# A pause in the routing of overflow and skip lists, and an earlier start of the row scales

## The chip, the core and the metric

The kernel runs on one core of a Trainium2 chip. Its engines work side by side, each through its own list of instructions in the order written: TensorE (PE, with its weight loads PEld), VectorE (DVE), ScalarE (ACT), GpSimd (POOL), and SyncE (SP), which issues most transfers. The metric is the device time of one execution in microseconds; lower is better.

## The reference

A causal filter of seven taps over `x` (4 sequences of 3584 tokens, 192 channels, one softmaxed filter per group of 24 channels) is followed by two mixtures of eight experts, each choosing one expert per token:

```python
x = attn_out.reshape(B * S, D)                 # 14336 rows of 192
do_compute = x @ w_skip > 0                    # layer 1 handles about half of the rows
xc = x[do_compute]
e_idx = np.argmax(xc @ w_gate, axis=1)
h = np.maximum(xc[mask] @ w1[e], 0.0)          # 192 -> 1024, per expert e
y[mask] = gate_w[mask, None] * (h @ w2[e])     # 1024 -> 192
out[do_compute] = xc + y                       # the other rows skip layer 1
logits = x @ w_gate + modality_bias[modality_id]
out[mask] = gate_w[mask, None] * (np.maximum(x[mask] @ w1[e], 0.0) @ w2[e])   # layer 2, all rows
```

## The kernel before

First a phase filters the tokens and computes the gates. Rows are then handled in **blocks** of 128 rows that share an expert: a block gathers its rows from DRAM by a list of indices, transposes them, and multiplies them with the expert's two weight matrices. Blocks 0 to 55 serve layer 1 from lists that are ready early; blocks 56 to 61 serve layer 1's overflow (rows of experts with more than 896 rows); then come blocks of layer 2, first those of the rows that skipped layer 1, then the rest.

`Ffn.run` writes the blocks one after another. In iteration i PE gets the two halves of the first product of block i (`mm1`, parts p0 and p1, 20 matmuls each into one bank) and then the second product of block i-1 (`mm2`, 24 matmuls). After each `mm1` part ACT writes `hh` (the relu, in 16 bits) and DVE writes `hlo` (what the 16 bits lost). After `mm2` DVE writes the row's result into `x2a` (blocks 0 to 15) or `x2s` (later ones). Once `late_pools` has run, some blocks earlier, three banks take turns for `mm1` (`m.ph`), two for `mm2`. So p1 of block b can only start when the `hlo` of p0 of block b-1 has been read out of the same bank, and `mm2` of block b-1, in iteration b, needs that block's second `hlo`.

Between these parts `bg(i, pt)` runs at four points of an iteration (pt 0, 2, 3, 4). It sets `step[0] = i` and calls `tick()` on three lists of background tasks. A task is a generator: `yield n` lets n ticks pass before its next piece is written into the engines' lists. The order on PE, DVE, ACT and POOL is the order of writing (`InOrder`); on SP a scheduler places the transfers. Background tasks in the blocks at issue:

- `route2` (list `tk`), on DVE but for a few matmuls. `ranks` counts skip rows by expert, `choose` ranks layer 2's experts (tile `sel`, on which the second conversion lane below waits). Then come the position arithmetic: `slots`, `left`, `place` (tiles `ns`, `sz`, `st`, `rC`, `pos`), `table` (`esl`, `tab`), the overflow positions (`codeA` with `rB`), `qsl` (`pi` to `q`), and `invert`, which turns positions into the index lists by comparisons (`oa`, `ob`) and groups of 8 matmuls. Its lists are needed from block 56 on.
- two lanes of `prep` (list `tkw`), which convert the next experts' weights to a 16-bit part and a 16-bit rest. DVE's shares are eight rows per expert: four 128x512 and four 128x384, written to `o` (layer 2) or `w1b`, `w2b` (layer 1).
- `scales` (list `tk2`): for each four blocks `scale2` has DVE find the rows' maxima (`mx` twice, `s`, `ef`), POOL scale two small tiles, and, four ticks later, ACT scale four tiles.

Of the kernel before, what the change touches and what calls it, by code (L numbers as in the profile page):

```python
# [30 lines left out]
EA = 4  # L31
SA = 3
SB = 7
NSA = E * SB
XA = 16
# [80 lines left out]
class Moe:  # L116
# [654 lines left out]
        for w in self.invert(S, q, sl, pool, ob, tag, res, lp, lag, base, val):  # L771
            yield w

    def route2(self, ra, pool, ob, l1, lb, lag):
        nc, cp = self.nc, self.cp
        code, rk = self.code[:, 0, :], ra["rk"]
        r, o, r1 = [], [], []
        for w in self.ranks(self.code[:, 1, :], pool, 1, r):
            yield w
        for w in self.choose(r[3], pool):  # L780
            yield w
        for w in self.slots(r[3], NP2B, True, pool, o):
            yield w
        self.left(r[3], NS2B, True, o, "B", pool, lb, cp)
        for w in self.place(r, NP2B, o, pool, 128.0 * NS1):
            yield w
        for w in self.table(NS2B, NP2B, o, "B", pool, ob, lb, cp, NSEL - 1):
            yield w
        lim = float(SB * 128)
        ov = pool.tile([128, 8], F32, name="th")  # L790
        nc.vector.tensor_scalar(ov, ra["base"], -lim, 0.0, ALU.add, ALU.max)
        for w in self.slots(ov, 0, False, pool, r1):
            yield w
        self.left(ov, NS1, False, r1, "1", pool, l1, cp)
        for w in self.table(NS1, 0, r1, "1", pool, ob, l1, cp):
            yield w
        of = pool.tile([128, 8], F32, name="dl")
        nc.vector.tensor_scalar(of, r1[1][:, 0], 128.0, 1.0 - lim, ALU.mult, ALU.add)
        df = pool.tile([128, 8], F32, name="sb")
        nc.vector.tensor_copy(df[:, 7:8], of[:, 7:8])  # L800
        nc.vector.tensor_tensor(df[:, 0:7], of[:, 0:7], of[:, 1:8], ALU.subtract)
        yield 1
        t = pool.tile([128, 2, NT], F32, name="rB")
        p1 = rk
        for e in range(8):
            nc.vector.scalar_tensor_tensor(t[:, e % 2], code, 8.0 - e, df[:, e:e + 1].to_broadcast([128, NT]), ALU.is_ge, ALU.mult)
            nc.vector.tensor_tensor(p1, p1, t[:, e % 2], ALU.add)
            if e % 2:
                yield 1
        nc.vector.scalar_tensor_tensor(p1, code, 0.0, p1, ALU.is_gt, ALU.mult)  # L810
        nc.vector.scalar_tensor_tensor(code, p1, 128.0 * NS1, code, ALU.is_gt, ALU.mult)
        nc.vector.scalar_tensor_tensor(p1, p1, 128.0 * NS1, p1, ALU.is_le, ALU.mult)
        nc.vector.tensor_tensor(p1, p1, o[4], ALU.add)
        yield 1
        q, sl = self.qsl(p1, pool)
        nc.gpsimd.memset(self.codeA[:, 0:NT], 0.0)
        yield 1
        res = {}
        for w in self.invert(NS1 + NS2B, q, sl, pool, ob, "m", res, cp, lag):
            yield w  # L820
        for l, a, b in ((l1, 0, NS1), (lb, NS1, NS1 + NS2B)):
            l.update(idx=res["idx"][:, a:b], va=res["va"][:, a:b])
# [477 lines left out]
def build(tc, x, cw, m1w1, m1w2, mod, bias2, m2w1, m2w2, wgs, out):  # L1300
    with ExitStack() as ctx:
        m = Moe(tc, ctx)
# [7 lines left out]
        rt = ctx.enter_context(tc.tile_pool(name="rt", bufs=1))  # L1310
        ob = m.oa = ctx.enter_context(tc.tile_pool(name="ob", bufs=4))
        pw = ctx.enter_context(tc.tile_pool(name="pw", bufs=2))
        pq = ctx.enter_context(tc.tile_pool(name="pq", bufs=4))
        la, ls, l1, lb, l2, lr = {}, {}, {}, {}, {}, {}
        ra = dict(a=la, s=ls)
# [12 lines left out]
        step, scaled = [-1], [0]  # L1328
# [25 lines left out]
        def routes():  # L1354
            while "idx" not in ls:
                yield 1
            va = m.cp.tile([128, NSA], F32, name="va")
            ra["va"] = va
            k = 0
            while k < NSA:  # L1360
                c = order[k][0] * SB + order[k][1]
                n = 1
                while k + n < NSA and order[k + n][0] * SB + order[k + n][1] == c + n:
                    n += 1
                nc.gpsimd.tensor_copy(va[:, k:k + n], ls["va"][:, c:c + n])
                k += n
                yield 1
            for i in m.route2(ra, rt, ob, l1, lb, 3):
                yield i

        tk, tk2, tkw = Tasks(), Tasks(), Tasks()
# [3 lines left out]
        def phase1():  # L1375
            v = next(gp, None)
            if v == 1:
                nc.sync.dma_start(rows[0:128, :], m.dz.bitcast(I32))
                nc.sync.dma_start(rows2[0:128, :], m.dz.bitcast(I32))
            if v == 2:  # L1380
                tkw.add(lane(0))
            if routed[0] < p1.codes:
                tk.add(m.route_a(routed[0], m.code[:, 0, :], rt, ob, ra))
                routed[0] += 1
            return v
# [17 lines left out]
        def late_pools():  # L1403
            st.close()
            m.py.append(m.py2)
            m.ph.append(m.ph3)
            px = ctx.enter_context(tc.tile_pool(name="px", bufs=1))
            w["x"] = px.tile([128, NC - XA, D], F32, name="x2s")
            po = sp.enter_context(tc.tile_pool(name="po", bufs=1))
            pw2 = sp.enter_context(tc.tile_pool(name="pw2", bufs=2))  # L1410
            w["pw2"] = pw2
            tkw.add(lane(1))
            o = po.tile([128, 4, F], F16, name="o1"), po.tile([128, W2C + 2], F16, name="o2")
            w["o"] = o
            tk.add(routes())
# [4 lines left out]
        def scales():  # L1420
            for c in range(0, NC, NB1):
                nb = min(NB1, NC - c)
                while step[0] < c + nb + 3:
                    yield 1
                for k in ffn.scale2(x2of(c, nb), mt[:, c:c + nb, :], nb):
                    yield k
                scaled[0] = c + nb

        def posts(par):
            for c in range(par * NB1, NC, 3 * NB1):  # L1430
                nb = min(NB1, NC - c)
                va = ra["va"][:, c:c + nb] if c < NSA else l1["va"][:, c - NSA:c - NSA + nb]
                while scaled[0] < c + nb:
                    yield 1
                for k in ffn.post(x2of(c, nb), mt[:, c:c + nb, :], nb, va, rows2[128 + c // GT * 2048:2176 + c // GT * 2048, :].rearrange("(p t) c -> p t c", p=128)[:, c % GT:c % GT + nb, :], m.codeA[:, c:c + nb]):
                    yield k
# [25 lines left out]
        def bg(i, pt):  # L1462
            step[0] = i
            if "x" not in w:
                phase1()
                if p1.codes == NG:
                    while phase1() is not None:
                        pass
                    late_pools()
            if i == XA and pt == 0:  # L1470
                tk2.add(scales())
            if i == n1 - 6 and pt == 4:
                tk.drain()
                tkw.drain()
                sp.close()
                ffn.pg = ctx.enter_context(tc.tile_pool(name="pg", bufs=2))
                ffn.pw = pw
                m.ph.pop()
                ffn.late = ctx.enter_context(tc.tile_pool(name="pl", bufs=4))
            if i == n1 + 2 and pt == 0:  # L1480
                tk.add(posts(0))
            if i == n1 + 4 and pt == 2:
                tk.add(posts(1))
            if i == n1 + 6 and pt == 4:
                tk.add(posts(2))
            if n1 + 7 < i < n2 - 6 and not tk.live and "idx" not in l2:
                tk.add(m.route(m.codeA[:, 0:NC], NS2A, "2", rt, ob, l2, np=NP2A, perm=True, top=NSEL - 1))
            if i == n2 and pt == 0:
                w["any"] = m.cp.tile([128, 1], I32, name="any")
                nc.vector.tensor_tensor(w["any"], l1["nrem"], lb["nrem"], ALU.add)  # L1490
                for v in (l2["nrem"], lb["un"], l2["un"]):
                    nc.vector.tensor_tensor(w["any"], w["any"], v, ALU.add)
                nc.vector.tensor_scalar(w["any"], w["any"], 1, None, ALU.min)
            if i == n2 - 6 and pt == 0:
                tk.drain()
                if "idx" not in l2:
                    tk.add(m.route(m.codeA[:, 0:NC], NS2A, "2", rt, ob, l2, np=NP2A, perm=True, top=NSEL - 1))
                    tk.drain()
            if i < n2:
                for _ in range(2 if i < EA * SA and "idx" not in ls else 1):  # L1500
                    tk.tick()
                tkw.tick()
                tk2.tick()
# [79 lines left out]
```

## Time and profile before

| | |
|---|---|
| median of three runs | 1000.76 us (1000.63 to 1001.26) |
| profiled execution: time, span of the core | 1001.09 us, 999.3 us |
| busy: PE, DVE, POOL, ACT | 917.8, 591.2, 512.7, 475.5 us |
| mean granted clock of TensorE | 0.967 |

Busy time is the sum of an engine's instructions; PE's matmuls are pipelined, so a busy PE is one that has no gap, not one at its peak. The profiled execution stands 0.33 us above the median of the runs. On DVE an instruction's end is recorded a little after the next one has begun, so what an instruction takes from the engine is read from start to start. Times in the trace count from the start of the span.

### The profile page before, as it was taken

What the parts mean: (1) busy time and instruction counts of PE and PEld (TensorE: products, weight loads), DVE (VectorE), ACT (ScalarE), POOL (GpSimd) and SP (SyncE); (2) the same over time, 40 slices, a digit from 0 to 9 for tenths busy, and PEclk for the clock granted to TensorE, in tenths of its full rate; (3) what the DMA queues carried; (4) which work ended last, traced back from release to release, by engine and by line L of the source; (5) the groups of instructions that cost most, each with busy time, mean ns of one, the idle gap of its engine ahead of it and who ended that gap; (6) DMA issues with size and microseconds to landing.
All of it is one profiled execution on the core that took longest, in us unless ns stands there. A gap on an engine that the chain in (4) does not pass through costs nothing. (4 is left out here: it accounts for less than half of the span.)

```text
span 999.3 us, 28862 instructions
## 1 busy us (share of the span) xinstructions
PE 917.8 (92%) x11000; PEld 852.6 (85%) x11000; DVE 591.2 (59%) x1624; ACT 475.5 (48%) x895; POOL 512.7 (51%) x985
## 2 busy tenths in 40 slices
PE   6999868997999999979999999999999999999993
PEld 4666668987999999968888898898888999999993
DVE  5689977899798877534455555477432333333330
ACT  3877743545686654324555555432233333333331
POOL 4155543742646355444768777644444555555431
PEclk9999859999999999999999999999999999999997
DMA  9595576764969776589333433322493232232240
GB/s 316 193 332 191 186 205 184 196 137 129 238 183 245 216 223 197 162 236 326 73 94 107 101 90 106 115 70 61 96 314 66 73 73 70 74 73 74 74 122 15
DMA packets 106196, 150.77 MB, mean 151 GB/s; under 512 B 80591, under 2 KB 85689, under 8 KB 100800
## 3 DMA queue, kind: packets, MB, share of 16 engines
q1 hardware_dynamic: 91424, 119.34, 38.8%
q0 software_dynamic: 13920, 28.87, 12.6%
q8 instruction: 88, 1.44, 0.6%
q14 instruction: 60, 0.49, 0.2%
q10 hardware_dynamic: 704, 0.63, 0.2%
HBM read 174.22 MB, written 51.08 MB: 225 GB/s over the span
## 5 line engine op out<-in xcount | busy, mean ns | idle before, releaser
L71 PEld LDWEIGHTS <-w1b 128*128 128x128 f16 x4840 | 371.4, 99 | 41.9 <-issue 13.5
L71 DVE SCALAR_TENSOR_TENSOR ws<-bank,ws 128x512 f16<-128x512 f32 x220 | 151.4, 690 | 262.1 <-ACT ws L71 215.1
L71 PE MATMUL bank<-xp,w1b 128*128 128x256 f16 x2200 | 266.5, 275 | 4.4 <-DMA xp<-gt 2.7
L71 PE MATMUL bank<-w2b,ws 128*128 128x192 f16 x2640 | 239.6, 246 | 0.1
L71 PEld LDWEIGHTS <-ws 128*128 128x128 f16 (+2 forms) x2696 | 223.6, 98 | 2.5
L71 POOL DMA_INDIRECT out_dram<-u,si x114 | 115.5, 1014 | 174.7 <-ACT ws L71 61.8
L71 ACT ACTIVATE ws<-bank 128x512 f16<-128x512 f32 x220 | 130.7, 598 | 105.5 <-PE bank L71 83.8
L71 PE MATMUL bank<-xt,w1b 128*128 128x128 f16 x2640 | 165.7, 223 | 11.5 <-DVE hlo L71 7.3
L71 ACT ACTIVATE hh<-bank 128x512 f16<-128x512 f32 x132 | 78.4, 594 | 151.7 <-PE bank L71 145.5
L71 PE MATMUL bank<-w2b,hh 128*128 128x192 f16 x1056 | 140.4, 249 | 4.7 <-DMA w2b<-s2a 3.5
L71 PE MATMUL bank<-w2b,hlo 128*128 128x192 f16 x528 | 131.4, 249 | 0.6 <-DVE hlo L71 0.6
L71 ACT ACTIVATE u<-bank,c 128x192 f32<-128x192 f32 x114 | 48.1, 422 | 165.3 <-PE bank L71 139.8
L71 DVE SCALAR_TENSOR_TENSOR hlo<-bank,hh 128x512 f16<-128x512 f32 x132 | 89.9, 684 | 56.5 <-ACT hh L71 51.3
L71 PEld LDWEIGHTS <-hh 128*128 128x128 f16 x1056 | 95.9, 100 | 5.4 <-issue 5.1
L71 POOL DMA_INDIRECT gt<-rows,idxm x62 | 62.4, 1007 | 10.8 <-issue 6.4
L71 POOL TENSOR_TENSOR xs<-gt 128x128 f32<-128x128 f16 x124 | 53.0, 449 | 27.8 <-DVE x2a L71 13.0
L71 POOL DMA_INDIRECT gt<-rows,idx x58 | 57.4, 989 | 14.3 <-issue 8.1
L71 PE MATMUL bank<-xg,band 128*112 128x384 f32 x128 | 58.1, 542 | 1.6 <-DVE hl L71 1.6
L71 ACT COPY xtb<-bank 128x672 f16<-128x672 f16 x64 | 45.9, 719 | 18.8 <-PE bank L71 18.6
L71 POOL TENSOR_SCALAR ef<-ef 128x4 f32<-128x4 f32 (+1 forms) x16 | 4.4, 276 | 97.3 <-DVE ef L71 97.2
L71 PEld LDWEIGHTS <-hlo 128*128 128x128 f16 x528 | 52.3, 99 | 1.6 <-DVE hlo L71 0.8
L71 POOL DMA_INDIRECT gt<-rows,idxs x44 | 47.3, 1075 | 6.7 <-POOL c L71 4.1
(293 smaller groups left out, 1137.2 us busy)
## 6 DMA issues: line engine op xcount, KB each, us to landing
w1b<-s1b SPq DMA_DIRECT2D x59, 1024.0 KB
w2b<-s2b SPq DMA_DIRECT2D x59, 768.5 KB
xg<-in_x_dram SPq DMA_DIRECT2D x7, 1536.0 KB
rows<-hl SPq DMA_DIRECT2D x7, 1386.0 KB
ws<-in_moe_w_dram SPq DMA_DIRECT2D x12, 768.0 KB
s1a<-w1b SPq DMA_DIRECT2D x8, 1024.0 KB
w1b<-s1a SPq DMA_DIRECT2D x7, 1024.0 KB
s2a<-w2b SPq DMA_DIRECT2D x8, 768.5 KB
```

Source lines behind the costliest of these rows:

```text
L71: r = f(*args, **kw)
```

## The change

`route2` stops between `choose` and `slots`: it yields once per tick until block 13 is reached. `scales` is added to its list at block 12 (`EA * SA`) rather than 16 (`XA`). Nothing is added to or taken from the work.

```diff
-    def route2(self, ra, pool, ob, l1, lb, lag):
+    def route2(self, ra, pool, ob, l1, lb, lag, step):
...
         for w in self.choose(r[3], pool):
             yield w
+        while step[0] < 13:
+            yield 1
         for w in self.slots(r[3], NP2B, True, pool, o):
             yield w
...
-            for i in m.route2(ra, rt, ob, l1, lb, 3):
+            for i in m.route2(ra, rt, ob, l1, lb, 3, step):
...
-            if i == XA and pt == 0:
+            if i == EA * SA and pt == 0:
                 tk2.add(scales())
```

DVE's list before, where `choose` ends and `slots` begins (`sel` is the last row of the one, `ns` the first of the other; the `x2a` row is the result of block 8, written in iteration 9):

```order
L71 TENSOR_REDUCE key<-rB 128x8
L71 TENSOR_SCALAR sel<-key 128x8
L71 TENSOR_SCALAR ns<-off 128x8
L71 TENSOR_SCALAR ns<-ns 128x8 x2
L71 CAST sz<-ns 128x8
L71 TENSOR_TENSOR sz<-ns 128x8
L71 TENSOR_TENSOR rB<-gt_3236,sz 128x64 x2
L71 SCALAR_TENSOR_TENSOR x2a<-bank_60,c,xs 128x192
```

DVE's list now, from the result of block 10 on (the first `hlo` row here belongs to block 12, the last one to p0 of block 13):

```order
L71 SCALAR_TENSOR_TENSOR x2a<-bank_60,c,xs 128x192
L71 SCALAR_TENSOR_TENSOR hlo<-bank_58,hh 128x512
L71 TENSOR_REDUCE mx<-x2a 128x4
L71 SCALAR_TENSOR_TENSOR hlo<-bank_59,hh 128x512
L71 TENSOR_SCALAR mx<-mx 128x4
L71 TENSOR_SCALAR s<-mx 128x4
L71 TENSOR_SCALAR ef<-mx 128x4
L71 SCALAR_TENSOR_TENSOR x2a<-bank_64,c,xs 128x192
L71 SCALAR_TENSOR_TENSOR hlo<-bank_63,hh 128x512
L71 TENSOR_SCALAR ns<-off 128x8
L71 TENSOR_SCALAR ns<-ns 128x8 x2
L71 CAST sz<-ns 128x8
```

`ns` follows `sel` at once before; now it stands behind the first `hlo` of block 13, four blocks later, and a group of scale rows stands in block 12.

The other end of the position arithmetic, on DVE before (the `hlo` row is p1 of block 16; `o` is a row of weight conversion):

```order
L71 SCALAR_TENSOR_TENSOR hlo<-bank_58,hh 128x512
L71 SCALAR_TENSOR_TENSOR codeA<-code,codeA 128x128
L71 SCALAR_TENSOR_TENSOR code<-codeA,code 128x128
L71 SCALAR_TENSOR_TENSOR codeA<-codeA 128x128
L71 TENSOR_TENSOR codeA<-codeA,pos 128x128
L71 SCALAR_TENSOR_TENSOR o_2517<-ws_3331,wsc,o_2517 128x2x192
```

and now (the first `hlo` row is p0 of block 20, the second p1; the `x2s` row is the result of block 18):

```order
L71 SCALAR_TENSOR_TENSOR x2s<-bank_60,c,xs 128x192
L71 SCALAR_TENSOR_TENSOR codeA<-code,codeA 128x128
L71 SCALAR_TENSOR_TENSOR code<-codeA,code 128x128
L71 SCALAR_TENSOR_TENSOR codeA<-codeA 128x128
L71 TENSOR_TENSOR codeA<-codeA,pos 128x128
L71 SCALAR_TENSOR_TENSOR hlo<-bank_59,hh 128x512
L71 TENSOR_SCALAR pi<-codeA 128x128
L71 TENSOR_SCALAR si<-pi 128x128
L71 TENSOR_SCALAR sl<-si 128x128
L71 TENSOR_SCALAR pi<-pi 128x128
L71 CAST q<-pi 128x128
L71 SCALAR_TENSOR_TENSOR hlo<-bank_63,hh 128x512
```

Before, the arithmetic runs from iteration 9 to iteration 17 and three conversion rows lie within it. Now it runs from iteration 13 to iteration 20. From the `hlo` of p0 of block 13 to that of p0 of block 20, both included, DVE's list now holds all position arithmetic up to the last `codeA` row, 15 `hlo` rows, 7 rows of `x2a` and `x2s`, eight conversion rows of 128x512 and eight of 128x384 (two whole experts), and three groups of scale rows. The conversions stand in the same blocks as before. The first group of `invert` matmuls on PE moves from iteration 20 to 24; there are 16 groups in either kernel.

## Rows read from the trace of the kernel before

**Rows 1.** Busy time by stretch: start and end, length, busy time per engine, granted clock, DMA.

```profile
190.00:262.00 72.00, 64.08 (x916) 63.00 (x917) 67.70 (x202) 36.80 (x64) 31.78 (x74) 0.98 0.67 179
250.00:425.00 175.00, 175.00 (x2549) 175.00 (x2547) 137.29 (x298) 103.52 (x194) 94.10 (x216) 1.00 0.74 209
```

**Rows 2.** Waits from 193 to 262 us: us in total, times, longest.

```profile
POOL ef L71 <- DVE ef L71: 20.5, 3, 12.1
...
PE bank L71 <- DVE hlo L71: 7.9, 5, 3.9
```

**Rows 3.** Timeline of PE: start, length, operation, count, wait ahead of it.

```profile
193.43 2.40 PE L71 MATMUL bank<-xt,w1b 128*128 128x128 f16 x40
197.65 2.40 PE L71 MATMUL bank<-xt,w1b 128*128 128x128 f16 x40
...
210.78 1.28 PE L71 MATMUL bank<-xt,w1b 128*128 128x128 f16 x20
...
242.12 1.28 PE L71 MATMUL bank<-xt,w1b 128*128 128x128 f16 x20 [3.92 <-DVE hlo L71]
...
246.87 2.40 PE L71 MATMUL bank<-xt,w1b 128*128 128x128 f16 x40
...
256.23 1.28 PE L71 MATMUL bank<-xt,w1b 128*128 128x128 f16 x20
257.35 1.08 PE L71 MATMUL bank<-ob,oa 128*128 128x62 f16 x8
258.25 1.30 PE L71 MATMUL bank<-xt,w1b 128*128 128x128 f16 x20
```

**Rows 4.** Timeline of DVE, same columns.

```profile
195.38 0.69 DVE L71 SCALAR_TENSOR_TENSOR hlo<-bank,hh 128x512 f16<-128x512 f32 x1 [0.59 <-ACT hh L71]
...
197.96 0.16 DVE L71 TENSOR_SCALAR ns<-off 128x8 int32<-128x8 f32 x1
...
237.12 0.61 DVE L71 SCALAR_TENSOR_TENSOR o<-ws,wsc,o 128x384 f16<-128x384 f32 x1
237.65 0.16 DVE L71 TENSOR_SCALAR mx<-mx 128x4 f32<-128x4 f32 x1
...
238.00 0.22 DVE L71 TENSOR_SCALAR pi<-codeA 128x128 int32<-128x128 f32 x1
...
239.23 0.61 DVE L71 SCALAR_TENSOR_TENSOR o<-ws,wsc,o 128x384 f16<-128x384 f32 x1
...
241.39 0.68 DVE L71 SCALAR_TENSOR_TENSOR hlo<-bank,hh 128x512 f16<-128x512 f32 x1
241.99 0.80 DVE L71 SCALAR_TENSOR_TENSOR o<-ws,wsc,o 128x512 f16<-128x512 f32 x1
242.71 0.68 DVE L71 SCALAR_TENSOR_TENSOR hlo<-bank,hh 128x512 f16<-128x512 f32 x1
...
262.37 0.42 DVE L71 SCALAR_TENSOR_TENSOR x2s<-bank,c,xs 128x192 f32<-128x192 f32 x1 [0.86 <-POOL c L71]
```

**Rows 5.** DVE's groups by form, 197.96 to 237.12 us: count, busy us, mean ns, idle.

```profile
L71 DVE SCALAR_TENSOR_TENSOR hlo<-bank,hh 128x512 f16<-128x512 f32 x14 | 9.5, 680 | 0.0
L71 DVE SCALAR_TENSOR_TENSOR x2a<-bank,c,xs 128x192 f32<-128x192 f32 x7 | 2.9, 411 | 0.0
...
L71 DVE SCALAR_TENSOR_TENSOR o<-ws,wsc,o 128x512 f16<-128x512 f32 x2 | 1.5, 746 | 0.0
...
L71 DVE TENSOR_REDUCE mx<-x2a 128x4 f32<-128x768 f32 x1 | 0.9, 943 | 0.0
L71 DVE SCALAR_TENSOR_TENSOR o<-ws,wsc,o 128x384 f16<-128x384 f32 x1 | 0.6, 609 | 0.0
```

**Rows 6.** The stretch with the lowered clock, columns as in the first group.

```profile
240.00:250.00 10.00, 7.88 (x95) 7.60 (x95) 9.97 (x20) 5.12 (x9) 4.51 (x10) 0.83 0.75 247
```

**Rows 7.** PE's waits for transfers from 425 to 465 us, around blocks 57 to 61.

```profile
PE bank L71 <- DMA xt<-gt: 4.1, 2, 2.5
PE bank L71 <- DMA w2b<-s2a: 3.5, 2, 2.6
```

## The prediction

> **What bounds the kernel now.** I read the busy time by stretch first. From 250 to 425 us PE has no gap at all, 175.00 us busy in 175 [rows 1]: there the kernel costs what its matmuls cost, and whatever is late at 250 is as late at 425. From 190 to 262 us it is different. PE is busy for 64.1 of 72 us and DVE for 67.7 [rows 1]. The waits of that stretch say why: PE waited five times for DVE's `hlo`, 7.9 us together [rows 2]. The timeline of DVE then shows how full it is: after a wait of 0.59 us ahead of the `hlo` row at 195.38, the next idle time that it names comes ahead of the row at 262.37 [rows 4]. Between these, DVE is the bound, and a stretch of its list takes as long as its rows take.
>
> A block costs PE 4.22 us (193.43 to 197.65, the starts of two blocks) [rows 3]. DVE's own share of a block, two `hlo` rows of 0.60 us from start to start (241.39 to 241.99 [rows 4]) and one `x2a` row of at most 0.41 us [rows 5], is 1.6 us. So about 2.6 us per block are free on DVE for the background, and the question is what each block gets.
>
> **What the change moves.** Nothing is added or removed; two pieces of DVE work change place. The position arithmetic leaves iterations 9 to 12 and starts in iteration 13, and the scale groups start four blocks earlier. The weight conversions stay where they are, from iteration 14 on. So the pause takes work off four blocks in which DVE had little else, and lays it over blocks that already carry two experts' conversions and now three groups of scale rows. I price the new stretch as one sum, from the `hlo` of p0 of block 13 to that of p0 of block 20, because the order shows that it ends with the last `codeA` row just ahead of that `hlo`.
>
> The base is the trace's own stretch from the `ns` row at 197.96 to the `o` row at 237.12 [rows 4]: 39.16 us without idle time, in which all the position arithmetic ran, with 14 `hlo`, 7 `x2a`, three conversion rows and one `mx` row among it [rows 5]. The new stretch has the same arithmetic and the same 7 results. It differs by:
>
> - one more `hlo` (15 for 14): +0.6 us;
> - six more conversion rows of 128x512 (eight for two) at 0.72 us (241.99 to 242.71) and seven more of 128x384 (eight for one) at 0.53 us (237.12 to 237.65) [rows 4]: 4.3 + 3.7 = +8.0 us;
> - scales: three groups, each an `mx` of 0.94 us [rows 5] and three small rows of 0.35 us (237.65 to 238.00 [rows 4]), less the one `mx` in the base: 3.9 - 0.9 = +2.9 us. With rows from start to start it would be a little less, so I take 2.7.
>
> Sum: 39.2 + 0.6 + 8.0 + 2.7 = 50.5 us.
>
> **From DVE's sum to PE's time.** Up to block 13 PE had no wait for DVE: it starts block 13 at 210.78 [rows 3], and the pause changes nothing ahead of that but makes DVE lighter. With DVE no longer behind, the first `hlo` of a block starts 1.95 us after the block (195.38 against 193.43 [rows 3, 4]), so the stretch starts at 212.7 and ends at 212.7 + 50.5 = 263.2. What it holds up is p1 of block 21, which uses the same bank. Before, such a start followed its `hlo` by 0.13 us (242.12 after 241.99 [rows 3, 4]), so p1 of block 21 starts at 263.3.
>
> Before, p1 of block 21 started at 258.25. But two groups of `invert` matmuls had run by then (iterations 20 and 21 to 22) that now come later, 0.90 us each (257.35 to 258.25 [rows 3]). They must still be done, so the fair mark is 258.25 - 1.8 = 256.45, and the delay is 263.3 - 256.45 = 6.9 us. The second `hlo` of block 20 stands five `pi` to `q` rows later, 1.23 us (238.00 to 239.23 [rows 4]) plus its own 0.60; PE needs only 1.12 us (256.23 to 257.35 [rows 3]) before it wants it for `mm2`. That adds 0.7. After this DVE's list is light (the `invert` rows with a block of `hlo`, no conversion until iteration 23), so the sum ends: **+7.6 us**.
>
> Sorted by PE: before, it lost 7.9 us waiting and 1.65 us at the lowered clock (half of `mm1` and `mm2` took 4.75 us, 242.12 to 246.87, where 4.22 - 1.12 = 3.10 is normal [rows 3]). Now it loses about 17 us, all of it between block 15 or 16 and block 21, and none in blocks 12 to 14.
>
> What costs nothing: the earlier scale rows on ACT, busy for 36.8 of 72 us [rows 1]; and POOL's `ef` rows, which wait for DVE and hold up the gathers behind them. POOL once stood 12.1 us for one `ef` [rows 2], and no wait of PE for a gather shows in that stretch; if that cover were gone, a gather late by 2 us would cost 2 us once. The end of `invert` moves from iteration 44 to 47, with its lists first wanted around iteration 52: five blocks, some 21 us, of slack.
>
> Both ends of what I can't see: the rows of the sum, priced by one row of their kind each, might be off by 1 us together either way; the clock could fall again in the last of the waits, +1.65 us; and part of the loss may be absorbed by the waits for transfers after 425 us, 4.1 + 3.5 = 7.6 us [rows 7]. I take none of these, since PE's releases of weight buffers start those transfers, so they move with PE. The likeliest case reaches from +4.5 to +10.
>
> **Time.** The profiled execution took 1001.09 us, 0.33 over the median, so 1001.1 + 7.6 = 1008.7 there, and 1000.76 + 7.6 = **1008.4 us** as a median.
>
> **Rivals.**
>
> *Faster: the pause clears the waits and the stacked work finds room.* For it: the first of the five waits fall into blocks that get lighter. The decision point is the price of the stretch: at 50.5 - 7.6 = 42.9 us the kernel stays the same, below it gains, at most the 7.9 + 1.65 = 9.6 us that are lost now, which gives 991.2. Against it: the position arithmetic alone with its blocks' own rows took 39.2 us in this trace without a gap, and the eleven us added to it are rows with prices. Chance 6%.
>
> *No change: the loss is taken back.* If the transfers waited for after 425 us were on their way regardless of PE, a PE that comes 7.6 us late would find them landed, and the 7.6 us of waits [rows 7] would go: 1000.8. Against it: in the code each of these weight loads goes into a buffer that an earlier block must have left. Chance 9%.
>
> *Worse: the clock.* In the stretch from 240 to 250 us, after the longest waits, the granted clock was 0.83, a mix of the two levels of 1.2 and 2.4 GHz; between 250 and 425 us, with PE always busy, it was 1.00 [rows 1, 6]. In the new stretch PE would be at work only some 60% of the time for about 40 us. If it ran at 1.2 GHz through blocks 16 to 21, a block would take 8.44 us, more than the 7.2 us that DVE takes (50.5 over seven blocks). Six such blocks from 223.4 (210.78 + 3 x 4.22) end at 274.0, where the forecast has block 22 start at 267.2 (263.3, 1.12, 0.7 and `mm2`, 4.22 - 2 x 1.12 = 2.0): 6.8 us more, 1015.2. Against it: a PE at 1.2 GHz would be the slower engine, would have no waits and, as after 242, get its clock back. Chance 10%. The Trainium skill (TensorE: Matmul & The Clock Gate, What's actually happening) says that the throttled clock is the default and that activity releases it, which is the rule behind this rival; this trace agrees as far as it goes, with 0.83 after waits and 1.00 in unbroken work.
>
> The pause doing nothing is excluded by the order, in which `ns` stands four blocks later.
>
> **How the numbers follow.** 0.2% is 2.0 us, about what a measurement of this kernel can tell from no change. The forecast has 72%, the clock 10%, no change 9%, faster 6%, and 3% stay for a partial loss under 2 us or a partial gain. Slower by over 0.2%: 72 + 10 and a little, 84%; within 0.2%: 9%; faster: 7%. The range 1003.5 to 1012.0 holds the forecast with its bounds (1005.3 to 1010.8) and some of a partial absorption or of a clock that stays low for two or three blocks; the rest, about 2 in 10, is left out.
>
> **What the new profile would show.** PE without a wait for `hlo` from 193 to about 222 us; from there to about 266 us a row of waits for `hlo`, two per block, most of 0.5 to 3 us, about 17 us together (less where the clock falls). DVE with idle time in blocks 9 to 12 and none from 213 to about 266. Block 22 starting near 267, where 258.25 + 1.12 + 2.0 gives 261.4 before. PE full from there to about 432, and the same waits of 7 to 8 us for transfers after it, 7 to 8 us later. I would be wrong if DVE has idle time between 215 and 260, if the waits after 425 shrink by what was lost before, or if the clock is 0.5 for more than a few us there.

## The result, and the profile after

The changed kernel is slower, by more than forecast. Its six runs took 1010.96 to 1020.35 us, with a median of 1017.17 us; the kernel before took 1001.14 us beside them (median of six). The ratio, formed like all ratios here from undisturbed runs (which leaves out one run of `a_half`), is 1.0145 with a 95% interval of 1.0111 to 1.0178, which is 14.5 us; the forecast was 7.6 us, in a range that ended at 1012.0. Runs of one kernel on one chip spread by about 1% here (988.63 to 998.69 us in 23 runs of the kernel before), and chips differ by as much (medians of the kernel before from 993.26 to 1004.48 us), so a kernel is compared only with the kernel before measured beside it. The change was measured three more times: 1.0130 (1.0093 to 1.0166), 1.0135 (1.0102 to 1.0167) and 1.0107 (1.0064 to 1.0150).

The profiled execution took 1014.88 us, with a span of 1013.1 us and a mean granted clock of 0.965 (0.967 before). The busy time by stretch answers to [rows 1] and [rows 6], with the same columns:

```profile
190.00:262.00 72.00, 58.69 (x844) 57.46 (x845) 61.11 (x182) 34.95 (x64) 26.92 (x68) 0.98 0.59 157
212.00:264.00 52.00, 36.69 (x515) 35.46 (x513) 49.83 (x150) 24.80 (x45) 19.10 (x45) 0.96 0.47 122
250.00:260.00 10.00, 9.62 (x121) 9.27 (x119) 9.69 (x31) 1.79 (x3) 0.00 (x0) 0.83 0.83 229
260.00:270.00 10.00, 6.11 (x74) 5.92 (x72) 9.68 (x27) 7.46 (x15) 7.83 (x17) 0.83 0.91 294
270.00:430.00 160.00, 159.12 (x2299) 158.76 (x2297) 123.47 (x265) 90.33 (x164) 79.82 (x183) 1.00 0.66 191
```

PE is busy for 58.7 of 72 us where it was busy for 64.1. From 212 to 264 us DVE is busy for 49.8 of 52 us and PE for 36.7: DVE is the bound there; from 270 to 430 us it is PE again, busy for 159.1 of 160 us. The clock is lowered in two slices, where it was in one. The waits of PE from 193 to 300 us, and from 425 to 465 us, answer to [rows 2] and [rows 7]:

```profile
PE bank L71 <- DVE hlo L71: 15.5, 7, 3.9
PE bank L71 <- DVE wsc L71: 0.5, 1, 0.5
...
PE bank L71 <- DMA w2b<-s2a: 3.2, 2, 2.2
PE bank L71 <- DMA xt<-gt: 2.7, 2, 2.5
PE bank L71 <- DMA w1b<-s1b: 0.2, 1, 0.2
```

The waits for `hlo` have gone from 7.9 to 15.5 us. Those for transfers are 6.1 us in place of 7.6 here, but 8.1, 5.7 and 8.4 us in three further traces of the changed kernel and 7.6 us in a second one of the kernel before: they did not shrink as a rule. Where the waits stand is in PE's timeline (to [rows 3]):

```profile
226.65 1.28 PE L71 MATMUL bank<-xt,w1b 128*128 128x128 f16 x20 [1.66 <-DVE hlo L71]
...
234.53 1.28 PE L71 MATMUL bank<-xt,w1b 128*128 128x128 f16 x20 [3.51 <-DVE hlo L71]
...
249.51 1.86 PE L71 MATMUL bank<-xt,w1b 128*128 128x128 f16 x20 [2.42 <-DVE hlo L71]
254.25 2.40 PE L71 MATMUL bank<-xt,w1b 128*128 128x128 f16 x40
...
264.19 2.29 PE L71 MATMUL bank<-xt,w1b 128*128 128x128 f16 x20 [3.89 <-DVE hlo L71]
268.66 2.40 PE L71 MATMUL bank<-xt,w1b 128*128 128x128 f16 x40
```

The first wait is that of p1 of block 16, the last that of p1 of block 21, and block 22 starts at 268.66. Before, it started at 261.37:

```profile
261.37 1.84 PE L71 MATMUL bank<-xt,w1b 128*128 128x128 f16 x30
```

Behind the last wait 20 matmuls took 2.29 us where 1.28 is usual, in a slice with a granted clock of 0.83. From 249.51 to 254.25 are 4.74 us where 3.10 are usual, in the other such slice. That the clock fell because PE had stood is tested below. DVE's timeline has both ends of the stretch that the prediction summed (to [rows 4]):

```profile
212.60 0.69 DVE L71 SCALAR_TENSOR_TENSOR hlo<-bank,hh 128x512 f16<-128x512 f32 x1 [0.51 <-ACT hh L71]
...
263.46 0.68 DVE L71 SCALAR_TENSOR_TENSOR hlo<-bank,hh 128x512 f16<-128x512 f32 x1
264.06 0.21 DVE L71 TENSOR_SCALAR pi<-codeA 128x128 int32<-128x128 f32 x1
...
432.63 0.69 DVE L71 SCALAR_TENSOR_TENSOR hlo<-bank,hh 128x512 f16<-128x512 f32 x1 [0.52 <-ACT hh L71]
```

From the row at 212.60 on, the next idle time that the timeline of DVE names is 0.87 us ahead of a row at 270.82. From 212.60 to 264.06 are 51.46 us (50.5 in the sum), with the rows that the sum counted (to [rows 5]):

```profile
L71 DVE SCALAR_TENSOR_TENSOR hlo<-bank,hh 128x512 f16<-128x512 f32 x15 | 10.2, 681 | 0.5 <-ACT hh L71 0.5
...
L71 DVE SCALAR_TENSOR_TENSOR w1b<-ws,wsc,w1b 128x512 f16<-128x512 f32 x4 | 3.2, 794 | 0.0
L71 DVE SCALAR_TENSOR_TENSOR o<-ws,wsc,o 128x512 f16<-128x512 f32 x4 | 3.0, 753 | 0.0
...
L71 DVE TENSOR_REDUCE mx<-x2a 128x4 f32<-128x768 f32 x3 | 2.8, 946 | 0.0
```

The row at 432.63 is `hlo` of p0 of block 56, by which the same work is done in both kernels. **The mark of block 56** in what follows is the start of that row less the start of the `hlo` of p0 of block 8, ahead of anything that is changed. It stands at 231.12 us before and at 241.73 after: 10.61 us. The other rows of the two marks, two from before and one from after:

```profile
190.92 0.67 DVE L71 SCALAR_TENSOR_TENSOR hlo<-bank,hh 128x512 f16<-128x512 f32 x1
422.04 0.69 DVE L71 SCALAR_TENSOR_TENSOR hlo<-bank,hh 128x512 f16<-128x512 f32 x1 [0.52 <-ACT hh L71]
```

```profile
190.90 0.67 DVE L71 SCALAR_TENSOR_TENSOR hlo<-bank,hh 128x512 f16<-128x512 f32 x1
```

In three further traces of the changed kernel it is 10.68, 10.86 and 10.81 us, in a second one of the kernel before 0.03: unlike the whole time, this part repeats within 0.3 us.

### The profile page after: what moved, and what is told of

Its sections match the earlier page's. It is cut to its first block, busy times and chain, and to the rows that moved or that the text cites. A ratio compares the mean times of both kernels' runs of the same rounds, so it can differ in the third digit from the quotient of the medians.

```text
span 1013.1 us, 28858 instructions
## 1 busy us (share of the span) xinstructions
PE 921.4 (91%) x11000; PEld 855.4 (84%) x11000; DVE 593.2 (59%) x1624; ACT 475.2 (47%) x895; POOL 512.2 (51%) x985
## 5 line engine op out<-in xcount | busy, mean ns | idle before, releaser
L71 POOL DMA_INDIRECT gt<-rows,idxm x62 | 62.4, 1007 | 10.8 <-issue 6.2
```

The costliest lines, as they stand in the source:

```text
L71: r = f(*args, **kw)
```

## The experiments

All of them, with the mark of block 56 against the kernel before, the time (median, or a single run), that of the kernel before measured beside it, and the ratio:

| kernel | what it is | block 56, us | time | before | ratio (95%) |
|---|---|---|---|---|---|
| e1_pause_only | the pause alone | +9.04 | 1006.08 | 993.26 | 1.0126 (1.0089 to 1.0162) |
| e2_scales_only | the early scales alone | +3.78 | 999.04 | 993.26 | 1.0071 (1.0046 to 1.0096) |
| r_after | the changed kernel again | +10.68 | 1005.92 | 993.26 | 1.0130 (1.0093 to 1.0166) |
| p2b12 | no pause, half pace in blocks 12 to 25, scales from 24 | -6.47 | 989.21 | 993.26 | 0.9950 (0.9922 to 0.9977) |
| b_again | the kernel before again | +0.03 | 1003.66 | 1001.28 | single run |
| a_fill912 | changed, four DVE rows more in blocks 9 to 12 | +12.00 | 1016.62 | 1001.28 | single run |
| a_fill1720 | changed, four DVE rows more in blocks 17 to 20 | +12.68 | 1014.49 | 1001.28 | single run |
| a_warm | changed, matmuls in the waits | +9.75 | 1011.15 | 1001.28 | 1.0107 (1.0066 to 1.0147) |
| a_half | changed, route at half pace up to block 27 | +0.33 | 1008.07 | 1002.72 | 1.0035 (1.0006 to 1.0063) |
| v_p2b10 | no pause, half pace in blocks 10 to 25, scales from 24 | -4.61 | 999.02 | 1002.72 | 0.9971 (0.9947 to 0.9996) |
| v_p19 | the pause alone, until block 19 | +11.84 | 1020.96 | 1002.72 | single run |
| r2_after | the changed kernel again | +10.86 | 1014.51 | 1002.72 | 1.0135 (1.0102 to 1.0167) |
| b_delay22 | before, 190 matmuls more in blocks 22 to 31 | +13.24 | 1004.48 | 994.89 | 1.0098 (1.0067 to 1.0130) |
| b_delay44 | before, 190 matmuls more in blocks 44 to 53 | +10.65 | 1002.93 | 994.89 | 1.0080 (1.0045 to 1.0114) |
| r3_after | the changed kernel again | +10.81 | 1006.87 | 994.89 | 1.0107 (1.0064 to 1.0150) |
| v_p2b10m | v_p2b10, clearing of codeA later | -4.06 | 999.03 | 1004.48 | 0.9949 (0.9925 to 0.9973) |
| v_p2b10e | v_p2b10, clearing and ef rows later | -5.36 | 984.38 | 993.64 | 0.9909 (0.9877 to 0.9942) |

**Which edit.** Each half of the change alone (diffs from the changed kernel: first the pause is kept, then the scales), and the change again.

```diff
-            if i == EA * SA and pt == 0:
+            if i == XA and pt == 0:
```

> The pause until block 13 alone; the row scales begin at block 16 as before. Stacked rows (the ledger of DVE): two of the three scale groups leave the stretch from block 13 to block 20, so it is about 1.2 to 2.6 us shorter than in the changed kernel; block 22 starts near 267 us (268.66 with both edits) and the time is 1 to 3 us under that of the changed kernel of the same call, some 12 us over the kernel before. Rival, the earlier scales are the cause: the time is within 3 us of the kernel before.

```diff
-        while step[0] < 13:
-            yield 1
```

> The earlier row scales alone, no pause. Stacked rows: two scale groups of about 2 us each come into blocks 12 to 16, where DVE has the position arithmetic already and is behind; PE's waits for hlo grow by about 2 us and the time by 2 us, to 1003. Rival, the earlier scales are the cause of most of the loss: 1010 or more, with waits of ACT or POOL that the kernel before does not have.

> The changed kernel once more, for its spread. If its runs fall into two groups by themselves (1011 to 1015 and about 1020, as in the six runs so far), they do so again, with the mean granted clock lower by 0.006 to 0.01 in the upper group. Rival, the two groups were chance of one chip: one group near 1012 or near 1020.

The pause does most of it: 9.0 of 10.6 us at block 56, 1.6 us less than with both edits, as expected (1 to 3); over the whole program the two did not differ (1006.08 and 1005.92 us). The scales alone cost 3.8 us, more than the 2 us expected. In their traces PE waits for `hlo` for 14.0 and 10.2 us:

```profile
PE bank L71 <- DVE hlo L71: 14.0, 7, 3.4
```

```profile
PE bank L71 <- DVE hlo L71: 10.2, 5, 3.2
```

For the scales that is 2.3 us more than before, near the 2 us that were put for their rows, and the clock is lowered in two slices (0.83 from 230 to 240 us and from 240 to 250 us) where it was in one. PE waits for neither ACT nor POOL there. Over the whole program the scales alone cost 4.6 to 9.5 us by their interval, more than the 3.8 us at block 56; where the rest is lost was not traced. The two halves do not add up to the whole (12.8 us): both fill the same blocks. The two groups of times in the first six runs of the changed kernel (1011 to 1015 and about 1020 us) did not come again: 1003.69 to 1009.52 us without a gap.

**What a DVE row costs, by place.** Four rows more on DVE (in-place, without effect on the data):

```diff
+            if i in (17, 18, 19, 20) and pt == 0:
+                q = m.iq[:, 0:64, :].rearrange("p a b -> p (a b)")
+                nc.vector.scalar_tensor_tensor(q.rearrange("p (c t) -> p c t", c=4), m.identf.unsqueeze(1).to_broadcast([128, 4, 128]), 0.0, q.rearrange("p (c t) -> p c t", c=4), ALU.mult, ALU.add)
```

> The changed kernel with four rows of 128x512 more on DVE, one in each of the blocks 9 to 12; they leave their target as it was. Stacked rows: DVE stands idle there for about a microsecond per block, so rows of 0.7 us cost nothing: block 22 within 0.4 us of the changed kernel. Rival, DVE's total work sets the time: 2.9 us later.

> The changed kernel with the same four rows in the blocks 17 to 20. Stacked rows: DVE has no idle time there, so each row costs its price: block 22 is 2.7 to 2.9 us later than in the changed kernel, plus or minus a drop of the clock more or less (1.5 us). Rival, PE is held back by the clock or by something else than DVE: less than 1 us.

> The kernel before once more, for a trace from the chip of the other runs. All theories: waits for hlo near 8 us between 190 and 300 us, block 22 near 261 us, one drop of the clock in that stretch.

In blocks 17 to 20 the four cost 2.07 us at block 56 (12.68 - 10.61, one trace). In DVE's timeline the first of them takes 0.60 us from start to start, so their price is 2.4, not the 2.7 to 2.9 that was expected:

```profile
240.16 0.68 DVE L71 SCALAR_TENSOR_TENSOR iq<-identf,iq 128x512 f16<-128x512 f32 x1
240.76 0.21 DVE L71 TENSOR_TENSOR esl<-esl,e 128x56 f32<-128x56 f32 x1
```

In blocks 9 to 12 they cost 1.39 us, where nothing was expected. Three show no cost: PE's blocks 9 to 13 start as in the changed kernel (3.41 us later each, and so is block 8). The one in block 12 was not; it comes ahead of the `mx` row there, and DVE's first `hlo` of block 13 starts at 216.80, 0.79 us later than by that offset. So block 12, just ahead of the full stretch, had no room left. The direction is as expected, but the two placements differ by only 0.7 us, in one trace each.

**The clock in the waits.**

```diff
+                for _ in range({16: 24, 17: 48, 18: 24, 19: 24, 21: 48}.get(i, 0)):
+                    nc.tensor.matmul(self.m.spare, self.m.ident, self.m.ident, start=True, stop=True)
                 self.mm1(X[k], jb["b"], 2 * part + 1, H[k])
```

> The changed kernel with 24 or 48 matmuls of 128x128 on PE more (1.3 or 2.7 us by 0.056 us each), on a bank that nothing reads, ahead of p1 of the blocks 16 to 19 and 21, where the changed kernel waits 1.7 to 3.9 us: PE works through the waits, the waits end when they did. If the drops of the clock in that stretch (near 250 and 264 us, about 3 us together) come of PE's standing still, they go: the granted clock stays 1.00 from 220 to 280 us, block 22 starts 1.4 to 3 us earlier and the time falls by as much. Rival, the clock drops for another reason or at fixed times: the drops stay and block 22 is where it was or later.

Two slices of its trace, and from its timeline the last wait:

```profile
250.00:260.00 10.00, 8.13 (x121) 7.79 (x119) 9.65 (x33) 2.06 (x4) 0.14 (x1) 1.00 0.99 271
260.00:270.00 10.00, 8.78 (x141) 8.66 (x139) 9.76 (x25) 8.63 (x19) 8.06 (x19) 1.00 1.04 314
```

```profile
263.77 1.28 PE L71 MATMUL bank<-xt,w1b 128*128 128x128 f16 x20 [1.22 <-DVE hlo L71]
```

Where the changed kernel has 0.83 twice, the clock is 1.00: the drops came of PE's standing still. The Trainium skill (TensorE: Matmul & The Clock Gate, What's actually happening) says that the throttled clock is the default and that activity releases it; this pair of traces agrees. The gain is 0.86 us at block 56 (9.75 for 10.61), not 1.4 to 3. Inside the stretch that DVE bounds, a faster PE only reaches its next wait earlier, so what counts is the drop behind the last wait (0.65 us, see below). The second trace of the changed kernel, `r_after`, bears this out: it has a third, deeper drop, from 230 to 240 us, and its mark of block 56 is the same within 0.1 us (10.68).

```profile
230.00:240.00 10.00, 6.50 (x64) 6.15 (x62) 9.97 (x20) 3.65 (x5) 0.82 (x2) 0.68 0.30 74
```

**Place and density.** The pause alone until block 19, with the scales from block 16 again; and both edits with the route at half pace up to block 27.

```diff
-        while step[0] < 13:
+        while step[0] < 19:
```

> The pause alone, until block 19 in place of 13; scales from block 16. Stacked rows: nothing is in DVE's way before block 20, so block 22 starts 10 us earlier than in the kernel before (near 251 us); then the arithmetic meets the conversions of the blocks 20 to 29, PE waits some 17 us for hlo between blocks 21 and 29, and block 56 starts 7 to 10 us later than before. Rival, the place of the pause does not matter: block 22 is as late as in the changed kernel.

```diff
             for i in m.route2(ra, rt, ob, l1, lb, 3, step):
-                yield i
+                yield i * (2 if step[0] < 28 else 1)
```

> Both edits of the change, the pause until block 13 and the scales from block 12, and after the pause the route takes its ticks at half the pace until block 27. Stacked rows: the pause costs nothing in itself, only that its rows and the conversions stand in the same seven blocks; laid over some twelve blocks, the rows of the trace add up to waits for hlo of about 8 us in place of 15.5, block 22 starts near 254 us (261.4 before) with more of the invert groups still to come, and block 56 starts 1 to 2 us earlier than in the kernel before, where the changed kernel starts it 10.6 us later: the time is 996 to 1001 where the kernel before has 1000. Rival, work that starts late (the route from block 13) is late at its end too: the time is that of the changed kernel, 1010 or more, or worse, since the lists come another four blocks later.

With the pause until 19, block 22 starts at 250.87 (near 251 expected), and then the loss comes, among it a wait for the conversion's `wsc` that the sum had not named:

```profile
250.87 1.28 PE L71 MATMUL bank<-xt,w1b 128*128 128x128 f16 x20
255.54 1.60 PE L71 MATMUL bank<-xt,w1b 128*128 128x128 f16 x20 [3.38 <-DVE hlo L71]
...
270.96 0.98 PE L71 MATMUL bank<-sa,ones 128*128 128x2 f32 x4 [4.45 <-DVE wsc L71]
```

At block 56 this kernel is 11.84 us late (7 to 10 expected). So the loss moves with the arithmetic, to where it meets the next conversions; it does not belong to block 13. At half pace, with the same pause and the same scales, the loss at block 56 is 0.33 us in place of 10.61 (1 to 2 us of gain had been expected), and the waits for `hlo` are 6.9 us:

```profile
PE bank L71 <- DVE hlo L71: 6.9, 7, 1.9
PE bank L71 <- DVE o L71: 0.6, 1, 0.6
```

This fits the reading that the pause costs little by itself, and that its rows' standing close together is what costs. But one thing more differs in this kernel: its edit slows the route from its start, not only behind the pause, so `sel` stands in block 12 rather than 9 and the conversions that wait for it begin two blocks later (block 17 rather than 15). How much of the gain is theirs was not separated. In `p2b12` below, where the conversions stand as before and the arithmetic is spread over blocks 9 to 20, the waits for `hlo` are 2.1 us, though there the scales are out of the way. Over the whole program `a_half` is 3.5 us slower all the same (0.6 to 6.3); where the rest is lost, behind block 56, was not traced.

**Lateness by itself.** 190 matmuls more in the kernel before, nothing moved:

```diff
+                for _ in range(19 if 44 <= i < 54 else 0):
+                    nc.tensor.matmul(self.m.spare, self.m.ident, self.m.ident, start=True, stop=True)
```

> The kernel before, with 19 matmuls of 128x128 more in each of the blocks 22 to 31 (190 by 0.056 us, 10.6 us of PE's time, on a bank that nothing reads), where PE is the bound; no list, conversion or scale row moves. It puts PE 10.6 us late at block 56 as the changed kernel does, and nothing else. If what the changed kernel loses beyond these 10.6 us (some 2 us in three measurements) belongs to coming late as such, this kernel is 12 to 13 us slower too. If it belongs to the moved rows (lists and conversions that come later), this kernel is 10.6 us slower and no more. If the waits for transfers after 425 us take lateness back, it is less than 8 us slower.

> The same 190 matmuls in the blocks 44 to 53, close ahead of the waits for transfers. The same three readings: 12 to 13 us slower if lateness costs more than itself, 10.6 us if not, under 8 us if the transfers run on and are found landed.

> The changed kernel beside these two, on the same chip: 12 to 13 us slower than the kernel before, as in the measurements so far, with 10.6 us of it lost by block 56.

A plain delay of 10.65 us at block 56 is worth 8.0 us at the end (4.5 to 11.3); one that had grown to 13.24 us by then (a wait of 1.67 us for gathered rows at 383.51 among it) is worth 9.8 (6.7 to 12.9). What lies behind block 56 does not take a delay back as a whole; by the middle values some 3 us may go there, by the intervals anything from nothing to 6. The changed kernel beside them loses 10.7 us (6.4 to 14.9) with 10.8 us at block 56. So three of its four intervals hold what is lost at block 56, and the first begins just above it.

**The other direction.** No pause, the route at half pace from block 12 or 10 to 25, the scales from block 24:

```diff
             for i in m.route2(ra, rt, ob, l1, lb, 3):
-                yield i
+                yield i * (2 if 10 <= step[0] < 26 else 1)
...
-            if i == XA and pt == 0:
+            if i == XA + 8 and pt == 0:
```

> The opposite of stacking: no pause; from block 12 to block 25 the route of overflow and skip lists takes its ticks at half the pace, and the row scales begin at block 24, once it is through. Stacked rows: the same work lies over more blocks with room; PE's waits for hlo between blocks 9 and 24 fall from 7.9 us to about 4, block 48 starts about 8 us earlier and the time is 991 to 996. Rival, the loss of the changed kernel is due to route work that is late for what comes after it: this kernel is late too (its lists come some 8 blocks later than before) and loses, 1005 or more.

> The kernel before without a pause, with the route at half pace in the blocks 10 to 25 and the scales from block 24. Stacked rows: almost no wait for hlo is left (under 1 us of 7.9), block 56 starts 10 us earlier than in the kernel before, and with the one drop of the clock gone too the time is 10 to 12 us less, a ratio near 0.989. Rival, room given to PE in this stretch is taken back by the waits for transfers after 425 us: within 3 us of the kernel before.

Both are faster than both kernels. The first waits 2.1 us for `hlo` (about 4 expected) and starts block 48 8.0 us earlier, as expected; its gain is 6.5 us at block 56. The second has no wait for `hlo` left, as expected, but gains 4.6 us at block 56, not 10. This is what PE does at 255 us, and what POOL does there:

```profile
255.17 3.82 PE L71 MATMUL bank<-xt,w1b 128*128 128x128 f16 x40 [2.62 <-DMA xt<-gt]
```

```profile
258.41 0.20 POOL L71 MEMSET codeA<- 128x128 f32 x1 [6.86 <-DVE pi L71]
258.58 0.19 POOL L71 TENSOR_TENSOR c<-gt,w2b 128x1 f32<-128x1 f32 x1
259.12 1.00 POOL L71 DMA_INDIRECT gt<-rows,idxs  x1 [0.35 <-POOL c L71]
```

PE waits for rows that are not there yet (`xt`, the transposed rows), and then runs a block at the low clock (3.82 us for 2.40): 4.0 us together. A gather stands behind POOL's wait. Two kernels set out to take POOL's waits away, the second with `yield 6` in the first of these places:

```diff
         q, sl = self.qsl(p1, pool)
+        yield 4
         nc.gpsimd.memset(self.codeA[:, 0:NT], 0.0)
-        yield 1
```

> The half-pace kernel without a pause (blocks 10 to 25, scales from block 24), with POOL's clearing of codeA written four ticks later. In the trace of that kernel without this edit POOL stands 6.86 us at the clearing, for DVE's pi row, with two gathers queued behind it; PE then waits 2.62 us for xt at 255.17 and the clock drops behind it. Stacked rows, with the gather as what took the gain back: the wait of 6.9 us on POOL and PE's 2.6 us for xt go, the clock stays 1.00 there, block 56 starts 8 to 10 us earlier than in the kernel before (4.6 us without this edit) and the ratio is near 0.992. Rival, the gain is lost elsewhere: block 56 stays 4 to 5 us early and the ratio 0.997.

```diff
-        nc.gpsimd.tensor_scalar(ef, ef, 0.5, None, ALU.mult)
-        nc.gpsimd.tensor_tensor(mt[:, :, 0], ef, mt[:, :, 0], ALU.mult)
         yield 4
+        nc.gpsimd.tensor_scalar(ef, ef, 0.5, None, ALU.mult)
+        nc.gpsimd.tensor_tensor(mt[:, :, 0], ef, mt[:, :, 0], ALU.mult)
```

> The half-pace kernel again, with both rows of POOL that can wait for DVE behind a few blocks of delay: the clearing of codeA six ticks later, and the two small ef rows of a scale group four ticks after DVE's. With the clearing alone moved, POOL stood 9.6 us at the first ef row in the same place, and PE's wait of 2.5 us for xt stayed. Held-up gathers as the cause: POOL's waits of over 5 us between 225 and 270 us go, PE's wait for xt at 255 and the drop of the clock behind it go, block 56 starts 8 to 10 us earlier than in the kernel before and the ratio is near 0.991. Rival, the gathers are late for another reason: the wait for xt stays at 2.5 us and block 56 is 4 to 5 us early.

POOL's waits from 225 to 270 us, in the first and in the second of them, and PE's wait in the second:

```profile
POOL ef L71 <- DVE kf L71: 9.6, 1, 9.6
```

```profile
POOL xs L71 <- DVE wsc L71: 5.0, 1, 5.0
...
POOL ef L71 <- DVE kf L71: 3.0, 1, 3.0
```

```profile
258.26 3.91 PE L71 MATMUL bank<-xt,w1b 128*128 128x128 f16 x38 [2.82 <-DMA xt<-gt]
```

The expectation fell both times: POOL's longest wait is 9.6 and then 5.0 us, PE's wait for `xt` stayed at 2.5 and 2.8 us, block 56 is 4 and 5 us early. The order in time shows why: POOL's waits were not the cause. In the trace of `v_p2b10` POOL stands from 251.55 to 258.41 us, and PE's wait is over at 255.17, before the gather behind POOL's wait is issued at 259.12. In the other two traces POOL's long waits begin only after PE's wait has ended. What ended PE's wait, by the semaphore that it waited for, was the transposing transfer that SP issues at 245.74 (the first of these two), which landed at 255.13:

```profile
245.74 4.49 SPq L1031 DMA_TRANSPOSE xt<-gt  x2
```

```profile
240.00:250.00 10.00, 10.00 (x160) 10.00 (x158) 9.75 (x29) 6.88 (x13) 6.35 (x15) 1.00 0.98 279
```

It took 9.4 us from issue to landing (9.2 and 9.6 in the other two traces); in the same trace those issued at 212.66, 216.90 and 221.12 took 2.3 to 3.5. The share of time in which the DMA engines were busy was 0.98 around the slow one and 0.24 from 212 to 224 us. So PE met a slow transfer in a stretch where the transfers are dense; whether an earlier issue would end the wait was not tried. The last kernel is nevertheless the fastest against its neighbours, 0.9909, more than its 5.4 us at block 56 account for; what it gains behind block 56 was not traced to a place.

## Why the prediction was wrong in its size

**What bounds the kernel, and which way it goes:** right. PE has no wait for `hlo` until 225 us, DVE has no idle time from 213 to 270 us, the loss falls in blocks 16 to 21 (in seven waits, not two per block), and where the rows stand less dense it is nearly gone (0.33 for 10.61 us, with the reservation made above).

**The price of the stretch,** 50.5 us: 51.46, so 1.0 short, the bound named for the rows. Summed from start to start, the rows that were added took what was put for them (11.2 us for 11.3). The mis-sized term is the base, "the same arithmetic": its 92 rows took 24.3 us in their new place and 23.1 in the old one; why is open. With this p1 of block 21 starts at 264.19 instead of 263.3.

**The clock in the last wait,** "I take none of these": this step failed. A drop of the clock behind the longest wait was in the trace of before (0.83, 240 to 250 us), and the reason given for taking none, that transfers move with PE, does not bear on it. The drop came: block 21's second half and `mm2` took 4.47 us (264.19 to 268.66) where 1.12 + 0.7 + 2.0 = 3.82 had been put, 0.65 us more. With the 0.9 of the late start, block 22 starts 1.5 us later than forecast: 7.6 has become 9.1.

**"After this DVE's list is light, so the sum ends":** this step failed. Between block 22 and block 56 another 1.5 us are lost (10.6 for 9.1). A wait of 0.54 us for `wsc` at 280.25 and one of 0.35 us for `hlo` at 406.53 are 0.9 of it; the other 0.6 stands in no wait that the profile names. From block 22 to block 56 the `mm1` matmuls take 76.55 us from start to start where they took 75.97. The `invert` groups and the conversions of the next experts, both later relative to PE than before, share those blocks.

So up to block 56 the sum was 7.6 us and is 10.6: the mechanism stands, and three of its terms were too small by 0.9, 0.65 and 1.5 us. That alone would have given 1011.4 us, still within the range. What carried the six runs beyond it, to 14.5 us, came behind block 56, where the prediction put nothing; its cause stays open (below).

**The rivals.** Faster: excluded by the stretch, 51.46 us against the 42.9 of the decision point. No change through the transfers: the waits for them did not go (5.7 to 8.4 us in four traces, 7.6 before), and two plain delays of 10.65 and 13.24 us still cost 8.0 and 9.8 us at the end. The clock at 1.2 GHz through blocks 16 to 21: did not happen; 0.83 in two slices of 10 us (in `r_after` 0.68 in one more), and filling the waits gave back 0.86 us.

**What stays open.** The four ratios have a mean of 1.0129, about 13 us, and 10.7 of them are lost by block 56. Whether the other 2 us are the change's is not settled. `r2_after` was to tell: its ratio of 1.0135 is what had been put for a loss of 3 us or more behind block 56, but its trace took 578.2 us from there to the end, within what had been put for no such loss (577 to 580). The last measurement, `r3_after`, showed nothing lost there, and plain delays lost less at the end than at block 56. From block 56 to the end single traces take 577.3 and 580.3 us before, 571.7, 573.0, 578.2 and 580.5 us after, which goes with the chip rather than with the kernel.

## What to carry to other kernels

Work moved off blocks where an engine idles is only worth moving if the blocks that take it have the room: write down, block by block, what each engine's rows cost from start to start, and look at the densest run of blocks and not at the mean. The same pause with the route at half pace, and the conversions two blocks later, was 10 us better at block 56 than with the rows close together. When such a sum predicts a delay, carry it past the last wait too: the clock that falls in it, and what is lost in the blocks behind it, added 2 of 10 us.

## What the runs showed that was not expected

A drop of TensorE's clock within a stretch that DVE bounds cost almost nothing: taking all of it away, by matmuls in the waits, gained 0.86 us, where the changed kernel spends 1.6 us more at the low clock behind the wait at 249.51 alone (4.74 for 3.10). And the kernel whose PE no longer waited for DVE at all met a new wait at once, 2.6 us for transposed rows. POOL's wait of 6.9 us beside it looked like the cause and was not: the transfer had been issued 5.8 us before that wait began and took 9.4 us. Before an edit sets out to end a wait, the trace can tell when the thing waited for was issued, and whether the supposed cause came first.
